# Attention taken as 16 heads by 128 queries instead of 4 heads by 512, with every token tile's projections following it

## The chip, the cores and the metric

One core of a Trainium2 chip. The time is the device time of one execution in microseconds, taken over three runs of the kernel before (2699.6 to 2700.16, median 2700.0).

## The reference

Four residual layers on a sequence of 2048 tokens of width 576 with 32 heads of width 18: A, B, A, B, with the same weights in both rounds.

```python
def _A_ref(x, wq, wk, wv, wo):           # 32 query heads, one key head and one value head
    q = (x @ wq) as [32 heads, 2048, 18]; k = x @ wk; v = x @ wv
    p = softmax(einsum("bhqd,bkd->bhqk", q, k) * 18 ** -0.5)
    return einsum("bhqk,bkd->bhqd", p, v) as [2048, 576] @ wo

def _B_ref(x, wqkv, w_phi, wo):          # linear attention
    q, k, v = x @ wqkv, per head
    phi_q, phi_k = [softmax(q w_phi), softmax(-q w_phi)], the same for k
    kv = sum over the tokens of phi_k^T v;  z = sum over the tokens of phi_k
    return (phi_q kv) / (phi_q z + 1e-6) @ wo

for _ in range(2):
    x = x + _A_ref(layernorm(x)); x = x + _B_ref(layernorm(x))
```

## The kernel before

Each of the two rounds ("layer" 0 and 1 in the code) has three stages.

**Projections of A** (`next_queries`, `project_queries`): queries, keys and values of all tokens; the keys stay in SBUF (`kst`), the values too (`vst`), the queries go to DRAM (`qd`).

**Attention with a stream beside it** (`attend`, L862). A group is 4 heads by 512 queries; 32 groups in all, `NG` = 8 head groups for each of `NC` = 4 chunks of 512 tokens. A group runs over 16 key tiles of 128. For each key tile there are two units: a unit is two score products of TensorE (`score`, L504, two heads at once in two row groups, `sc` in PSUM) and one exp of 128x1024 on ScalarE (L964, `sc` to `pt`). Two units are followed by a sum, four products `pt` by `vst` into a PSUM bank (`add_values`, L800; the profile counts each of the four twice). So one layer has 1024 units and 512 sums. There are three `sc` buffers, and nine `pt`.

The order on TensorE and VectorE is the order in which the program was written: `in_order` (L948) pins both engines. The loop (L1017) has two modes. With work in `bulk` a turn writes three units, the sums that are ready, three more units, then a piece of bulk work (`fill`), then the sums again, unless the piece was heavy (`HEAVY`). Without bulk work it writes two units and one sum at a time. `tick` advances three queues by one step: `urgent` (finishing a group), `loads` (weights) and `slow` (spills of features); a turn with bulk work has three ticks, a free turn one tick for every two units.

Bulk work is B's part: for each chunk, when its last head group is done, `chunk_work` (L1206) multiplies the four token tiles with `wo` (`output`, two halves of 14 products), adds the residual, normalizes and flips each tile through DRAM (`flip_tokens`, `fetch_tokens`, `split_tokens`), and then `mix` takes keys, values and feature queries of each tile with `wk`, `wv` and `wpq` (two halves of 14 products each) and adds to the state (`update_state`, L580). I call such a half, 14 products of 288 columns at L239, a projection: 8 per tile. `wo` and `wpq` share one place in SBUF and are reloaded in turn for each chunk. In layer 0 `fold_phi` runs in the stream as well.

Finishing a group (`finish_group`, L887) takes the group's sums from PSUM (`turned`), divides, transposes back, splits into a high and a low part (`parts`) and packs both with SBUF-to-SBUF transfers into `on`, the stationary operand of the projection with `wo` (`pack`, L827; 4 to 8 transfers). The last group of a chunk then waits three ticks before `chunk_work` starts. Every DMA of the kernel is issued by SyncE (the queue is called SP below), in one order.

**The tail**: the last chunk's tiles. `last_group` finishes the last group with TensorE transposes and packs it, eight projections with `wo` follow (five begun with the products whose operand doesn't come from the last group), four `last_mix`, `finish_state`, and then for all 16 tiles `read_out` and, in layer 0, the projections of the next A.

## Time and profile before

| what | value |
|---|---|
| median of the three runs | 2700.0 us |
| span of the profiled execution | 2699.8 us |
| TensorE, ScalarE, VectorE busy | 2627.5, 2158.1, 1213.9 us |
| granted TensorE clock over the span | 0.994 |
| layer 0: attention to the end of its last sum, about | 136 to 1191 us |
| layer 1: attention to the end of its last sum, about | 1457 to 2517.6 us |
| tail of layer 1 | 2517.6 to 2699.8 us |

The profiled execution's own time is its span; it lies 0.2 us under the median of the runs. In the chain of waits most pieces are TensorE's, some are exps of ScalarE (L964). The rows of a timeline give the start, the length, engine and line, `out<-in`, a count of merged instructions, and in brackets how long the engine stood idle before it and for what. The rows of windows give for each engine the busy time with the number of instructions, then the granted TensorE clock (1.00 is full).

### The profile page before, as it was taken

The numbers are of one execution on the slowest core, as the hardware profiler recorded it, in microseconds if no ns is written. First come the engines' busy times: TensorE is split into PE (matmuls) and PEld (weight loads), VectorE is DVE, ScalarE is ACT, GpSimd is POOL, SyncE is SP. The second block draws the span as 40 slices with busy tenths as digits, with TensorE's granted clock in tenths as the row PEclk, the third lists the DMA queues.
The fourth block names the chain that finished last, engine by engine and source line by source line (L and its number), as shares of the span: only waits on it lengthen the run. The fifth ranks groups of instructions, "written<-read, shape, count | busy, mean of one in ns | idle before, by whom it ended". The sixth has DMA issues, their size and how long they took to land. (4 is left out here: it accounts for less than half of the span.)

```text
span 2699.8 us, 55195 instructions
## 1 busy us (share of the span) xinstructions
PE 2627.5 (97%) x22094; PEld 1444.8 (54%) x22094; DVE 1213.9 (45%) x2807; ACT 2158.1 (80%) x2551; POOL 75.6 (3%) x114
## 2 busy tenths in 40 slices
PE   7999999999999999999999999999999999999999
PEld 6633335453545454558996222455445544554788
DVE  8422244542454245437773111254525452545475
ACT  4599998999899989963335999999998999899421
POOL 1000000000000000002000000000000000000110
PEclk9999999999999999999999999999999999999999
DMA  6531254313421341136645210231224113412354
GB/s 184 163 121 54 65 166 153 93 28 86 119 49 35 84 122 45 38 97 193 185 134 177 71 28 23 55 111 38 58 73 117 41 32 99 118 36 71 108 162 136
DMA packets 353248, 254.30 MB, mean 94 GB/s; under 512 B 191770, under 2 KB 273882, under 8 KB 352986
## 3 DMA queue, kind: packets, MB, share of 16 engines
q1 hardware_dynamic: 352986, 250.71, 32.4%
q8 instruction: 176, 2.88, 0.5%
q14 instruction: 86, 0.70, 0.1%
HBM read 146.12 MB, written 83.69 MB: 85 GB/s over the span
## 5 line engine op out<-in xcount | busy, mean ns | idle before, releaser
L964 ACT ACTIVATE pt<-sc 128x1024 f32<-128x1024 f32 x2036 | 1915.9, 1112 | 155.9 <-PE sc L504 137.2
L504 PE MATMUL sc<-qst,kst 56*128 56x512 f32 x3840 | 712.6, 454 | 16.7 <-ACT pt L964 16.3
L504 PEld LDWEIGHTS sc<-qst,kst 56*128 56x128 f32 x3840 | 324.0, 184 | 618.1 <-ACT pt L964 573.9
L800 PE MATMUL acc<-pt,vst 128*32 128x512 f32 x4096 | 505.1, 599 | 0.0
L800 PE MATMUL ps<-pt,vst 128*32 128x512 f32 x4048 | 491.1, 600 | 1.4 <-DVE featk L536 1.4
L800 PEld LDWEIGHTS ps<-pt,vst 128*32 128x32 f32 x4048 | 105.7, 109 | 212.1 <-issue 206.4
L239 PE MATMUL ps<-wahi,xs 128*128 128x288 f32 x954 | 208.5, 305 | 0.9 <-ACT xs L137 0.7
L800 PEld LDWEIGHTS acc<-pt,vst 128*32 128x32 f32 x4096 | 103.3, 109 | 197.2 <-issue 191.5
L239 PEld LDWEIGHTS ps<-wahi,xs 128*128 128x128 f32 x954 | 157.6, 190 | 11.6 <-issue 3.9
L239 PE MATMUL ps<-walo,xs 128*128 128x288 f32 x530 | 156.2, 297 | 0.0
L889 DVE STREAM_TRANSPOSE turned<-acc 128x512 f32<-128x512 f32 x30 | 21.4, 714 | 217.5 <-PE acc L800 217.5
L388 PE MATMUL ps<-xsc,wbhi 128*128 128x256 f32 x576 | 107.7, 286 | 0.6 <-ACT xsc L137 0.6
L410 ACT ACTIVATE pc<-ps 128x256 fp32r<-128x256 f32 x80 | 30.4, 384 | 93.3 <-PE ps L388 89.2
L239 PEld LDWEIGHTS ps<-walo,xs 128*128 128x128 f32 x530 | 100.6, 190 | 0.0
L263 POOL TENSOR_TENSOR rstd<-var,neghalf 128x1 f32<-128x1 f32 (+1 forms) x56 | 32.0, 571 | 2439.9 <-DVE var L261 2417.7
L137 ACT ACTIVATE xs<-ps 128x512 fp32r<-128x512 f32 x40 | 23.8, 594 | 94.0 <-PE ps L282 93.9
L388 PEld LDWEIGHTS ps<-xsc,wbhi 128*128 128x128 f32 x576 | 91.5, 193 | 1.6 <-ACT xsc L137 1.1
L889 DVE STREAM_TRANSPOSE turned<-ps 128x512 f32<-128x512 f32 x32 | 22.9, 716 | 142.9 <-PE ps L800 142.9
L388 PE MATMUL ps<-xsc,wblo 128*128 128x256 f32 x320 | 86.1, 284 | 0.0
L239 PE MATMUL ps<-wchi,on 128*128 128x288 f32 x378 | 82.2, 303 | 0.0
L296 DVE TENSOR_TENSOR xc<-xc,ps 128x288 f32<-128x288 f32 x58 | 25.7, 445 | 123.4 <-PE ps L239 123.2
L536 DVE COPY featq<-acc 128x288 f32<-128x288 f32 x32 | 14.6, 457 | 123.0 <-PE acc L239 123.0
(257 smaller groups left out, 3200.8 us busy)
## 6 DMA issues: line engine op xcount, KB each, us to landing
qst<-qd SPq DMA_DIRECT2D x360, 72.0 KB
pht<-phi SPq DMA_DIRECT2D x32, 540.0 KB
qd<-pc SPq DMA_DIRECT2D x64, 256.0 KB
on<-parts SPq DMA_DIRECT2D x192, 72.0 KB
phi<-pht SPq DMA_DIRECT2D x96, 144.0 KB
wchi<-wod SPq DMA_DIRECT2D x35, 288.0 KB
wclo<-wod SPq DMA_DIRECT2D x35, 288.0 KB
wchi<-wpqd SPq DMA_DIRECT2D x35, 288.0 KB
```

The costliest lines, as they stand in the source:

```text
L137: A.activation(dst_hi, src, AF.Copy)
L239: T.matmul(dst, xs[:, slot, :], w[half][:, k, c0 : c0 + HALF], start=(n == 0), stop=(n == last))
L263: G.tensor_tensor(rstd, var, neghalf[:, :n], op=ALU.pow)
L296: V.tensor_add(xr, xr, po)
L388: T.matmul(po, lhs, xsc[:, slot, :], start=(n == 0), stop=(n == LASTP))
L410: A.activation(pc[:, 0, :], po, AF.Copy)
L504: T.matmul(sc, kst[head_rows(h), t * P : (t + 1) * P], q[head_rows(h), h // 2, :], start=True, stop=True)
L536: V.tensor_copy(e[:, hs, 0, :], src)
L800: T.matmul(acc[32 * j : 32 * j + 32, :], vst[:, t, :], pts[j], start=first, stop=last)
L889: V.transpose(turned, acc[c, g])
L964: A.activation(pt, sc, AF.Exp, scale=SCALE)
```

## The change

A group is now 16 heads by 128 queries: `NG` = 2 groups for each of 16 token tiles. The products and exps of a group keep their shapes, since four heads stand side by side in the 512 columns that held 512 queries. There are still 32 groups, 1024 units and 512 sums per layer. What differs:

- Query rows are loaded in runs of 128 tokens instead of 512 (`load_queries`, `load_shifts`), in the same number of transfers.
- Finishing a group no longer packs into `on`: `keep_group` writes the parts to DRAM (`od`, 8 transfers), and after a tile's second group `load_heads` reads the whole tile back as `on` (4 transfers), one tick later. Three ticks after that the tile is `finished`.
- `stream` replaces `chunk_work`: for each finished tile the two `wo` projections, the flip, and, once the tokens are there, the six projections of `mix`. When nothing is to be done it sets `idle`, and the loop runs in the free mode.
- `wo`, `wk`, `wv` and `wpq` have a place each, and nothing is reloaded during the attention.
- The last token tile's `wo` and the tiles that are not mixed by the end (`left`; 13, 14 and 15 in layer 0, 14 and 15 in layer 1) stay for the tail. Mixing in the attention starts only with more than `MIX` = 42 units left. So the attention of layer 0 now holds 30 projections with `wo` and 78 of `mix`, that of layer 1 30 and 84; before it was 24 and 72 in each.
- `last_group` packs 16 heads of 128 queries, a head at a time.

```diff
-NG = 8
-GH = H // NG
-NC = 4
+NG = 2
+GH = 4
+HG = H // NG
+HS = HG // GH
+CW = HS * P
...
+    def keep_group(parts, c, g):
+        for j in range(GH):
+            row = first_head(g, j) * DH
+            dst = ods[c % 2][:, row : row + HS * DH, :].rearrange("n (x d) t -> d n x t", d=DH)
+            for n in range(2):
+                nc.sync.dma_start(dst[:, n], parts[32 * j : 32 * j + DH, n, :].rearrange("d (x t) -> d x t", t=P))
+
+    def load_heads(on, c):
+        src = ods[c % 2]
+        for n in range(2):
+            nc.sync.dma_start(on[:, 5 * n : 5 * n + 4, :], src[n, :512].rearrange("(k p) t -> p k t", p=P))
+            nc.sync.dma_start(on[n * 64 : n * 64 + 64, 4, :], src[n, 512:])
...
     def pack(dst, src, g):
         for j in range(GH):
-            row = g * GW + j * DH
+            for x in range(HS):
+                row, cols = (first_head(g, j) + x) * DH, slice(x * P, (x + 1) * P)
...
-        groups = [(c, g) for c in chunks for g in (*range(NG - 2), NG - 1, NG - 2)]
+        groups = [(c, g) for c in range(NT) for g in range(NG)]
...
-                pack(on[c].bitcast(F32), parts.bitcast(F32), g)
-                for _ in range(3):
-                    yield STAGE
-                if g == NG - 2:
-                    bulk.append(after_chunk(c, on[c], Spare(), loads, slow))
+                keep_group(parts.bitcast(F32), c, g)
+                yield STAGE
+                if c == NT - 1 or g == NG - 1:
+                    while c > 0 and c - 1 not in st["added"]:
+                        yield STAGE
+                    on = heads_in()
...
+                    load_heads(on.bitcast(F32), c)
+                    for _ in range(3):
+                        yield STAGE
+                    finished.append((c, on))
...
             while at[0] < len(units):
-                if bulk:
+                if not st["idle"]():
...
                 else:
-                    for n in range(3):
-                        ready = scores(2)
-                        sums(min(ready - 1, done[0] + 2))
-                        tick()
+                    ready = scores(2)
+                    sums(min(ready - 1, done[0] + 2))
+                    tick()
+                    fill()
...
+                def finish_tile():
+                    i, on = finished.popleft()
...
+                    yield from output(i, on, ps)
+                    nc.sync.dma_start(xd[i], xres[i])
...
+                while v.left():
+                    if finished:
+                        yield from finish_tile()
+                    elif fetched is None and unflipped and v.left() > FLIP:
...
+                        flip_tokens(i)
+                        fetched = i, fetch_tokens(i)
+                        if xs is None:
+                            yield from rest(6)
+                            turn_tokens()
+                    elif xs is not None and v.left() > MIX:
...
+                        yield from mix(i, parts, st, ps, spills[layer], loads, slow, turn_tokens)
...
+            EARLY, LATE = range(6), range(6, len(PRODUCTS))
+            sums = [ps.tile([P, HALF], F32, name="ps") for b in range(2)]
+            for b in range(2):
+                run(project(sums[b], st["wo"], b * HALF, on, None, EARLY))
...
+            for b in range(2):
+                run(project(sums[b], st["wo"], b * HALF, on, None, LATE))
+                add_residual(c, b, sums[b])
```

TensorE before, in layer 1, from the last sums of the first chunk's last group (`acc` and `ps` are the two PSUM banks in turn) to the first projection with `wo` (`wchi,on`):

```order
L504 MATMUL sc<-qst,kst 128x512 x4
L800 MATMUL ps<-pt,vst 32x512 x4
L504 MATMUL sc<-qst,kst 128x512 x6
L800 MATMUL ps<-pt,vst 32x512 x8
L504 MATMUL sc<-qst,kst 128x512 x6
L239 MATMUL acc<-wchi,on 128x288
```

The same place after the change, for token tile 2 of layer 1; the row ahead of these is `L797 MATMUL acc`, the tile's last sum:

```order
L797 MATMUL ps<-pt,vst 32x512 x8
L510 MATMUL sc<-qst,kst 128x512 x6
L587 MATMUL acc<-featk,vb_17418 32x36 x32
L797 MATMUL ps<-pt,vst 32x512 x4
L510 MATMUL sc<-qst,kst 128x512 x6
L797 MATMUL ps<-pt,vst 32x512 x8
L510 MATMUL sc<-qst,kst 128x512 x6
L797 MATMUL ps<-pt,vst 32x512 x4
L510 MATMUL sc<-qst,kst 128x512 x6
L797 MATMUL ps<-pt,vst 32x512 x8
L510 MATMUL sc<-qst,kst 128x512 x6
L240 MATMUL acc<-wchi,on 128x288
```

The projection with `wo` now stands 15 units behind the last sum of every tile (`x6` is three units), with the state of the tile before (L587) between them, and it comes 15 times in a layer instead of once for a chunk.

SP's queue before, at the end of a chunk's head groups in layer 1 (`on<-parts` is the packing):

```order
L493 DMA qst<-qd_103 18x2x512 x6
L498 DMA qst<-mxd_105 2x2x512 x2
L836 DMA on<-parts 8x2x512
L839 DMA on<-parts 10x512 x2
L839 DMA on<-parts 18x512 x6
```

And after the change, around the end of a token tile in layer 1 (`od` is the tile's heads in DRAM, `phi<-pht` a spill of features):

```order
L829 DMA od_106<-parts 18x4x128 x8
L494 DMA qst<-qd_103 18x8x128 x6
L501 DMA qst<-mxd_105 2x8x128 x2
L829 DMA od_106<-parts 18x4x128 x8
L642 DMA phi_109<-pht 32x36x32
L834 DMA on<-od_106 128x4x128
L835 DMA on<-od_106 64x128
```

The heads now leave in eight transfers per group and come back in four (the last two rows stand twice in the queue), and a spill stands between the two.

SP's queue before, at the end of layer 0's attention (`on<-xs` packs the layer's last group):

```order
L635 DMA phi_106<-pht 32x36x32 x4
L628 DMA pht<-phi_106 108x10x128
L629 DMA pht<-phi_106 72x128
L836 DMA on<-xs 18x2x512 x4
L202 DMA wclo_13473<-wpqd 128x576
```

The same place after the change:

```order
L635 DMA pht<-phi_108 108x10x128
L636 DMA pht<-phi_108 72x128
L856 DMA on<-xs 10x128
L856 DMA on<-xs 18x128
L853 DMA on<-xs 18x2x128 x9
L853 DMA on<-xs 6x2x128
L853 DMA on<-xs 12x2x128
L853 DMA on<-xs 18x2x128 x2
L853 DMA on<-xs 8x2x128
L856 DMA on<-xs 10x128
L856 DMA on<-xs 18x128 x5
```

The packing of the last group went from 4 transfers to 22. On TensorE all 28 products with `wo` of the last tile stand ahead of the first transposes of `last_mix`.

## Prediction

> **What bounds the kernel now.** I read the page first, for the busy shares and the costliest group:

> ```profile
> PE 2627.5 (97%) x22094; PEld 1444.8 (54%) x22094; DVE 1213.9 (45%) x2807; ACT 2158.1 (80%) x2551; POOL 75.6 (3%) x114
> L964 ACT ACTIVATE pt<-sc 128x1024 f32<-128x1024 f32 x2036 | 1915.9, 1112 | 155.9 <-PE sc L504 137.2
> ```

> The exps fill 1916 us of the 2700, and they wait for scores for 137. So two engines share the bound, and I looked where which one sets the pace. The windows give a stretch with no projections, and the whole attention of layer 1:

> ```profile
> 1500.00:1690.00 190.00, 190.00 (x1248) 54.85 (x1240) 20.95 (x36) 190.00 (x209) 0.00 (x0) 1.00 0.09 25
> 1457.00:2517.60 1060.60, 1050.43 (x8248) 466.53 (x8246) 387.99 (x774) 986.13 (x1070) 6.48 (x12) 1.00 0.26 69
> ```

> In the free stretch ScalarE is never idle: 209 exps in 190 us, 0.909 us a unit. The timeline of ScalarE in a stretch with a projection in every turn, six units to a row:

> ```profile
> 1708.33 5.81 ACT L964 ACTIVATE pt<-sc 128x1024 f32<-128x1024 f32 x6 [0.19 <-PE sc L504]
> 1714.99 5.80 ACT L964 ACTIVATE pt<-sc 128x1024 f32<-128x1024 f32 x6 [0.84 <-PE sc L504]
> 1721.64 5.84 ACT L964 ACTIVATE pt<-sc 128x1024 f32<-128x1024 f32 x6 [0.85 <-PE sc L504]
> ```

> Six units and a projection take 6.65 us (1714.99 to 1721.64) against 5.45 for six free ones, and ScalarE now waits for TensorE. The chain of waits shows what TensorE does in such a turn, and the timeline a turn with a state update (its scores start at 1801.16, the next turn's at 1806.95):

> ```profile
> 1711.74 2.71 PE ps L800 x24
> 1715.35 2.05 PE acc L239 x14
> ```
> ```profile
> 1801.16 0.97 PE L504 MATMUL sc<-qst,kst 56*128 56x512 f32 x6
> 1802.06 0.76 PE L580 MATMUL ps<-featk,vb 128*32 128x36 f32 x63
> 1806.95 0.97 PE L504 MATMUL sc<-qst,kst 56*128 56x512 f32 x6
> ```

> Three sums 2.71 us (0.90 each), a projection 2.05, three scores about 0.90. A projection thus costs the attention 1.20 us, a state 5.79 - 5.45 = 0.34. Layer 1's 1060.6 us are 1024 x 0.909 + 96 x 1.20 + 12 x 0.34 = 1050 and 10 more: hardly a stall is left to remove.

> **More projections in the attention.** 108 + 114 instead of 96 + 96, and 13 + 14 states instead of 12 + 12: 30 x 1.20 + 3 x 0.34 = **+37.0 us**. Two thirds of the way lies beside exps already; 1.20 is what sticks out. A projection directly behind a free stretch isn't shown cleanly; its cost lies between nothing and 1.20, and I take the row's 1.20.

> **The tail has fewer tiles.** The chain at the end of layer 1:

> ```profile
> 2514.25 3.33 PE acc L800 x24
> 2520.55 14.94 PE ps L239 x112
> 2537.95 0.49 ACT xs L137
> 2538.48 9.24 PE ps L239 x56
> 2547.72 0.44 PE ps L282 x4
> 2548.16 0.11 PE ps L286
> 2588.59 0.46 DVE fmax L538
> 2590.07 0.36 DVE kv L586
> 2594.27 2.24 DMA kvb<-featk
> ```

> The last sum ends at 2517.58. The four tiles' mixes run from 2538.48 to 2588.59, 12.5 us a tile. One goes in layer 0, two in layer 1: **-37.6 us**. With fewer tiles side by side each hides less of its chain; I keep the 12.5.

> **The last group is packed in 22 transfers instead of 4.** SP's timeline:

> ```profile
> 2522.49 3.36 SPq L836 DMA_DIRECT2D on<-xs  x4
> ```
> ```profile
> 1543.73 2.12 SPq L493 DMA_DIRECT2D qst<-qd  x6
> 1552.12 3.37 SPq L836 DMA_DIRECT2D on<-parts  x4
> ```

> Before, eight projections (14.94 us) covered the packing, and the mixes began 20.9 us after the last sum. Now only 12 products can run without it, and 28 stand ahead of everything else on TensorE, which stands idle. SP starts 4.91 us after the last sum; 22 x 0.84 = 18.5; the last transfer lands 2.24 later (the kvb row); ten products at 14.94 / 112 = 0.133 make 1.3; then transposes and a copy (0.44 + 0.11 + 0.49) 1.05. That is 28.0, 7.1 later than before, twice: **+14.2 us**. If a transfer takes SP what a `qst` row takes (0.35), it is 17.3, and -7.2 in all.

> **The heads go through DRAM.** This is the new wait. The projection with `wo` is now queued a fixed number of units behind the tile's last sum, and behind it on TensorE stand all scores and sums, for which ScalarE waits. How soon can `on` be there? VectorE's rows for a group that ends in a busy turn, the values of a projection (L567) among them, then the rows of one that ends in a free stretch:

> ```profile
> 2143.73 0.72 DVE L889 STREAM_TRANSPOSE turned<-ps 128x512 f32<-128x512 f32 x1 [1.45 <-PE ps L800]
> 2146.66 0.46 DVE L567 COPY vb<-acc 128x288 f32<-128x288 f32 x1 [1.20 <-PE acc L239]
> 2148.87 0.70 DVE L901 STREAM_TRANSPOSE osb<-turned 128x512 f32<-128x512 f32 x1
> 2150.07 0.69 DVE L140 TENSOR_TENSOR parts<-osb,parts 128x512 fp32r<-128x512 f32 x1
> ```
> ```profile
> 1548.42 0.72 DVE L889 STREAM_TRANSPOSE turned<-ps 128x512 f32<-128x512 f32 x1 [25.67 <-PE ps L800]
> 1551.40 0.69 DVE L140 TENSOR_TENSOR parts<-osb,parts 128x512 fp32r<-128x512 f32 x1
> ```

> A free group has its parts 3.7 us after the last sum. In a busy turn L901 waits for the projection's own work on VectorE (2.2 us, from 2146.66 to 2148.87) and takes 1.9 with the split. Then SP and the way out and back, for which the flip of the tokens is the model:

> ```profile
> 1721.39 2.00 SPq L635 DMA_DIRECT2D flipped<-pht  x4
> 1724.95 0.40 SPq L649 DMA_DIRECT2D xn<-flipped  x1
> 1725.39 1.17 SPq L651 DMA_DIRECT2D xn<-flipped  x2
> ```

> Writes to DRAM at 0.50 each: eight are 4.0. The read was issued 1.56 after the last write's issue ended (1723.39). Four reads, 0.40 + 0.59 twice, 2.0; the last lands 2.2 later. Together 9.8 us from the parts to `on`. At a `qst` row's 0.35 a write it is 8.6, at an `on<-parts` row's 0.84 it is 12.5; the flip's rows are the nearest, since they go the same way.

> By the order (shapes of layer 1):
> - a state between sum and projection (tiles 1, 2, 5, 8, 11, 14): TensorE comes after 1.8 (two sums) + 5.79 + 5.45 + 0.9 = 13.9 us. VectorE waits for the state (3.5), adds it (0.36), splits (1.9): 5.8, with 9.8 and a spill queued ahead of the reads (0.6) 16.2. Wait 2.3.
> - a projection first (tiles 3, 4, 6, 7, 9, 10, 12, 13): TensorE after 0.9 + 6.65 + 5.79 + 0.9 = 14.2; the projection ends at 3.85, with 2.2 + 1.9 the parts are there at 8.0, `on` at 17.8. Wait 3.6.
> - tile 0, free: ten units, 9.1; `on` at 3.7 + 9.8 = 13.5. Wait 4.4.

> Layer 1: 6 x 2.3 + 8 x 3.6 + 4.4 = 47. In layer 0 eight tiles stand so close (4 and 12 like the second kind, 5 and 13 about 3.1, 6 like the third, 0, 1 and 2 behind `fold_phi` about 1, 1 and 3.4): 23; the others have 21 units and more. In hand ScalarE has three units (2.7) against the projection and its next score (2.3): 0.4 of each of the 23 waits is covered. 70 - 9 = **+61 us**.

> **The clock behind such a wait.** The windows around the first mix of the tail:

> ```profile
> 2535.50:2539.20 3.70, 1.70 (x10) 1.28 (x11) 2.99 (x13) 3.13 (x7) 1.66 (x3) 1.00 0.81 219
> 2539.20:2542.60 3.40, 3.40 (x16) 3.40 (x15) 1.12 (x5) 0.60 (x2) 0.54 (x1) 0.50 0.99 351
> ```

> TensorE was busy 1.70 of 3.70 us, and for the next 3.4 its granted clock was 0.50: 1.7 us lost. I count that for the waits of 3.4 and more (9 in layer 1, 4 in layer 0 with its tile 2): 13 x 1.7 = **+22 us**; its bounds are 0 and 23 x 1.7 = 39.

> Against it speaks the end of the mixes: TensorE stood idle through the 2.24 us of the kvb transfer, and the clock behind it stayed full:

> ```profile
> 2596.60:2699.80 103.20, 97.50 (x1254) 93.25 (x1254) 58.96 (x182) 16.06 (x41) 2.33 (x2) 1.00 0.50 156
> ```

> So the size of the gap alone doesn't decide, and 3.4 is my choice between the two.

> [...]

> At nothing I cost the waits for the flipped tokens (14 units, 12.7 us, for 4.1 + 2.0 + 1.6 + 1.6 + 2.2 + 1.6 on VectorE and the way through DRAM, 13.1: 0.4, which the units in hand cover), the finer query loads (29 us ahead of their use) and the weights that aren't reloaded, since no wait for them shows in the 1060.6.

> **The sum**, against the execution's own 2699.8: +37.0 - 37.6 + 14.2 + 61 + 22 = +96.6, so 2796.4; the runs' median is 0.2 above the span, 2796.6.

> **Rivals.**
> - *The clock stays up*: the waits end before half a stretch of 3.4 us is idle, as at the kvb transfer: as forecast without the 22, 2774. [...]
> - *The heads are in time*: `on` within 6.2 us of the parts (14.2 - 8.0). 2699.8 + 13.6 = 2713. For it: the loop has three ticks between read and use. Against it: out and back alone takes 1.56 + 2.2 and twelve issues.
> - *Dear small transfers*: 0.84 on the way out too. 2.7 more for 23 waits, ten more slow windows: 2796 + 62 + 17 = 2875.
> - *TensorE's spare time pays*, the one with a faster end. In free steps it waits for ScalarE, as the row of its weight loads shows:

> ```profile
> 1551.95 0.19 PEld L504 LDWEIGHTS sc<-qst,kst 56*128 56x128 f32 x2 [0.84 <-ACT pt L964]
> ```

>  0.84 for two units, 4.2 for the ten free units of a tile, more than the mean wait of 3.0. If waits fall into it, and the 28 projections that begin behind a free stretch cost nothing instead of 1.20 (34 us), the time is 2713 - 34 = 2679. It decides from the point where a wait and a projection fit into what ScalarE has in hand. Against it: that is three units, 2.7 us, not 4.2.
> - *The weights are still reloaded*: the order has each slab once in a layer, so no chance is kept for it.

> **How the numbers follow.** Chances: forecast 0.38, clock up 0.20, heads in time 0.14, dear transfers 0.08, spare time 0.15, and 0.05 for an end within 0.2%, about what a measurement of this kernel can tell from no change, between the last ones. Slower by over 0.2%: 0.80; within: 0.05; faster: 0.15. The range of 2680 to 2855 leaves out the dear transfers and half of the spare-time case; the forecast's own range is 2760 to 2835 by the bounds of the writes.

> **What would show it.** Waits of TensorE at the first `wo` product of a tile, for a DMA, 2 to 4.5 us long, some 23 of them; granted clock 0.5 after the long ones; 222 projections in the attention, with ScalarE's gaps up by 1.2 for each new one; some 17 us of idle TensorE at the end of each attention; two mixes in layer 1's tail. Wrong I'd be if `on` is there before TensorE, or if the exps don't pause while it waits.

## The result, and the profile after

The changed kernel takes 2848.5 us (four runs, 2847.9 to 2852.8), the kernel before 2700.1 on the same chip: a ratio of 1.055 (95% interval 1.0535 to 1.0565). The forecast was 2796.6 with a range of 2680 to 2855. The sign was right and the time lies in that wide range, but it is 52 us over the forecast and outside the forecast's own range of 2760 to 2835. The profiled execution has a span of 2847.1 us, 147.3 more than that of before.

First the busy shares, ScalarE's group and two groups of projections on the page of the changed kernel (busy time, mean ns; then idle time ahead of them and what ended it):

```profile
PE 2667.7 (94%) x22046; PEld 1474.3 (52%) x22046; DVE 1249.2 (44%) x2852; ACT 2147.3 (75%) x2521; POOL 61.6 (2%) x102
L988 ACT ACTIVATE pt<-sc 128x1024 f32<-128x1024 f32 x2036 | 1920.1, 1047 | 310.5 <-PE sc L510 294.6
L240 PE MATMUL ps<-wahi,xs 128*128 128x288 f32 x1035 | 236.7, 315 | 27.5 <-DVE xs L133 23.7
L240 PE MATMUL acc<-wchi,on 128*128 128x288 f32 x477 | 115.4, 327 | 34.8 <-DMA on<-od 33.9
```

The exps' own time hardly moved (1915.9 to 1920.1), but they wait for TensorE's scores for 295 us instead of 137. TensorE has two new waits: 34 us for the heads (`on`), which was forecast, and 24 us for the flipped tokens (`xs`), which was costed at nothing. The windows of layer 1: attention, the tail up to its first mix, the mixes, the rest:

```profile
1511.90:2680.80 1168.90, 1106.58 (x8635) 516.53 (x8630) 439.79 (x884) 994.03 (x1080) 8.11 (x15) 0.98 0.24 61
2680.80:2708.90 28.10, 10.59 (x42) 8.76 (x42) 5.38 (x14) 1.79 (x5) 1.17 (x2) 0.61 0.19 60
2708.90:2744.70 35.80, 31.99 (x333) 30.55 (x335) 24.28 (x56) 11.70 (x23) 9.30 (x8) 0.88 0.70 213
2744.70:2847.10 102.40, 97.39 (x1232) 93.27 (x1232) 56.34 (x176) 12.79 (x34) 0.00 (x0) 0.97 0.51 157
```

Layer 1's attention, taken here from its first exp (1455.0 before, 1511.9 now), went from 1062.6 to 1168.9 (+106), its tail from 182.2 to 166.3 (-16). In layer 0 the attention grew by 61, and the stretch up to layer 1's first exp fell by 4. Sum: +147.

To see where the 106 and the 61 lie I went through all exps of a layer. By how much the distance from one start to the next exceeds the free unit's 0.909 us is put down to the projection (or state update) that TensorE ran last. The table has these sums in us, with the number of projections; the columns after the second belong to the experiments below. In the traces of both kernels the first six exps of each layer stand under names of weight tiles (`wchi<-sc` to `walo<-sc`); they start 0.90 to 0.92 us apart and add nothing.

| excess over 0.909 a unit | before | changed | e1 | e2 | e3 | e5 | e6 | e8 | e11 |
|---|---|---|---|---|---|---|---|---|---|
| layer 1, first `wo` projections (15) | - | 44.0 | 44.1 | 89.6 | 18.9 | 64.1 | 40.2 | 25.3 | 42.2 |
| layer 1, first mix projections (14) | 13.2 (12) | 74.4 | 108.4 | 16.8 | 67.7 | 17.2 | 52.7 | 15.9 | 41.2 |
| layer 1, all | 130.5 | 236.5 | 272.3 | 222.6 | 204.3 | 198.4 | 209.2 | 156.4 | 200.2 |
| layer 0, all | 147.5 | 208.7 | 206.3 | 208.1 | 191.8 | 190.9 | 207.8 | 185.2 | 209.6 |

Layer 1 adds up: 130.5, 18 more projections and two states (22.3), 44.0 - 15 x 1.20 = 26 at the heads, 74.4 - 14 x 1.20 = 58 at the tokens: 236. So more than half of layer 1's loss lies at a place that the forecast had at nothing.

A tile with such a wait. VectorE, SP and TensorE of the changed kernel (each row: start, length, then in brackets the idle time before it and its end):

```profile
1913.17 0.72 DVE L907 STREAM_TRANSPOSE turned<-ps 128x512 f32<-128x512 f32 x1 [7.50 <-PE ps L797]
...
1916.14 0.69 DVE L134 TENSOR_TENSOR parts<-osb,parts 128x512 fp32r<-128x512 f32 x1
1916.75 0.42 DVE L133 CAST xs<-xn 128x512 fp32r<-128x512 f32 x1
```
```profile
1909.33 0.39 SPq L656 DMA_DIRECT2D xn<-flipped  x1
1909.76 2.10 SPq L658 DMA_DIRECT2D xn<-flipped  x2
```
```profile
1917.32 0.37 PE L240 MATMUL ps<-wahi,xs 128*128 128x288 f32 x1 [2.38 <-DVE xs L133]
...
1920.53 1.65 PE L510 MATMUL sc<-qst,kst 56*128 56x512 f32 x6
```

The tokens' reads are issued by 1911.86. But VectorE works in written order, to which `in_order` pins it, and the split of the tokens is written behind the finishing of the head group: it idles 7.50 us until the group's last sum, takes 3.6 for the group, and only then turns to the tokens. And the projection takes 3.2 us to the next scores, not 2.05, most of it the clock's doing (with the clock kept up it is 2.5, e4 below). Three windows around the wait:

```profile
1912.00:1915.40 3.40, 2.94 (x22) 0.69 (x20) 2.13 (x4) 3.40 (x5) 0.00 (x0) 1.00 0.36 105
1915.40:1918.80 3.40, 1.35 (x8) 1.14 (x9) 2.82 (x7) 0.74 (x1) 0.00 (x0) 0.99 0.19 47
1918.80:1922.20 3.40, 3.40 (x18) 2.38 (x21) 1.49 (x4) 0.77 (x1) 0.00 (x0) 0.51 0.47 128
```

TensorE was busy 1.35 of 3.40 us, and the next window runs at half clock (0.51).

### The profile page after: what moved, and what is told of

Its sections match the earlier page's. It is cut to its first block, busy times and chain, and to the rows that moved or that the text cites. A ratio compares the mean times of both kernels' runs of the same rounds, so it can differ in the third digit from the quotient of the medians.

```text
span 2847.1 us, 55572 instructions
## 1 busy us (share of the span) xinstructions
PE 2667.7 (94%) x22046; PEld 1474.3 (52%) x22046; DVE 1249.2 (44%) x2852; ACT 2147.3 (75%) x2521; POOL 61.6 (2%) x102
## 5 line engine op out<-in xcount | busy, mean ns | idle before, releaser
L988 ACT ACTIVATE pt<-sc 128x1024 f32<-128x1024 f32 x2036 | 1920.1, 1047 | 310.5 <-PE sc L510 294.6
L797 PE MATMUL acc<-pt,vst 128*32 128x512 f32 x4096 | 498.6, 602 | 6.1 <-DVE xc L297 3.3
L797 PE MATMUL ps<-pt,vst 128*32 128x512 f32 x4048 | 497.0, 603 | 0.0
L240 PE MATMUL ps<-wahi,xs 128*128 128x288 f32 x1035 | 236.7, 315 | 27.5 <-DVE xs L133 23.7
L797 PEld LDWEIGHTS acc<-pt,vst 128*32 128x32 f32 x4096 | 107.3, 109 | 226.7 <-issue 214.7
L797 PEld LDWEIGHTS ps<-pt,vst 128*32 128x32 f32 x4048 | 105.9, 110 | 215.4 <-issue 210.9
L240 PEld LDWEIGHTS ps<-wahi,xs 128*128 128x128 f32 x1035 | 177.2, 197 | 55.9 <-issue 25.2
L240 PE MATMUL ps<-walo,xs 128*128 128x288 f32 x575 | 174.5, 305 | 0.0
L240 PE MATMUL acc<-wchi,on 128*128 128x288 f32 x477 | 115.4, 327 | 34.8 <-DMA on<-od 33.9
L297 DVE TENSOR_TENSOR xc<-xc,acc 128x288 f32<-128x288 f32 x53 | 23.9, 451 | 252.8 <-PE acc L240 252.8
L240 PEld LDWEIGHTS acc<-wchi,on 128*128 128x128 f32 x477 | 83.2, 202 | 59.5 <-issue 25.9
L240 PEld LDWEIGHTS ps<-walo,xs 128*128 128x128 f32 x575 | 113.6, 198 | 0.0
L240 PE MATMUL ps<-wbhi,xs 128*128 128x288 f32 x486 | 107.0, 305 | 0.0
L574 DVE COPY vb<-ps 128x288 f32<-128x288 f32 x44 | 20.1, 458 | 186.2 <-PE ps L240 186.2
L240 PEld LDWEIGHTS ps<-wbhi,xs 128*128 128x128 f32 x486 | 79.6, 188 | 16.1 <-issue 15.7
```

What stands on the lines that cost most here:

```text
L240: T.matmul(dst, xs[:, slot, :], w[half][:, k, c0 : c0 + HALF], start=(n == 0), stop=(n == last))
L297: V.tensor_add(xr, xr, po)
L797: T.matmul(acc[32 * j : 32 * j + 32, :], vst[:, t, :], pts[j], start=first, stop=last)
L988: A.activation(pt, sc, AF.Exp, scale=SCALE)
```

## The experiments

All are edits of the changed kernel, timed beside the kernel before. Theory A: TensorE's waits for heads and tokens, with the clock behind them, are the loss. Rivals: the waits only change places; the flip's way through DRAM is too long by itself; something else of the tail or the queries costs.

**e1: query loads with the eighth key tile.**

```diff
-if t == 0 and hh == 0 and 0 < n < len(groups) - 1:
+if t == 8 and hh == 0 and 0 < n < len(groups) - 1:
```

> Of the changed kernel only the place moves where a group's query loads are issued: with the group's eighth key tile, not with its first; the order on TensorE is the same, row for row. Queue theory: in layer 1 ten of fourteen tiles keep TensorE waiting 1.9 to 3.0 us at their first mix product (excess over ScalarE's pace about 6.0 us each), because the eight query loads (some 2.9 us of SP) and the writes of the heads stand between the flip's writes and its reads; in the four tiles where they stand behind, the wait is 0.66 and the excess 3.2. Without the loads in the way the ten come down to the four: 10 x 2.8 = 28 us less, about 2820 (2812 to 2830). Path theory (the rival): the flip's own way through DRAM is longer than the twelve units that are left to it, whatever else SP does: the waits stay and the time is 2848 within 5.

Measured: 2877.5 (ratio 1.066, 1.064 to 1.067), 29 slower. Both expectations fell. SP and TensorE in a tile of e1:

```profile
1906.89 1.99 SPq L642 DMA_DIRECT2D flipped<-pht  x4
1909.66 0.28 SPq L494 DMA_DIRECT2D qst<-qd  x1
1917.31 0.27 SPq L829 DMA_DIRECT2D od<-parts  x1
1917.76 0.38 SPq L656 DMA_DIRECT2D xn<-flipped  x1
```
```profile
1921.30 0.58 PE L240 MATMUL ps<-wahi,xs 128*128 128x288 f32 x1 [5.19 <-DVE xs L133]
```

With the loads moved, a write of the heads stands ahead of the tokens' reads in SP's order. It waits for VectorE's parts, and SP stands for 7.4 us with the reads behind it. The edit hadn't only taken something out of the queue; it changed what stands where.

**e2: a tile is mixed when the next tile's tokens have been asked for.**

```diff
-elif xs is not None and v.left() > MIX:
+elif xs is not None and v.left() > MIX and (fetched is not None or v.left() < FLIP):
...
-yield from wait(lambda: not finished and v.left())
+yield from wait(lambda: not finished and v.left() and not (xs is not None and MIX < v.left() < FLIP))
```

> A tile is mixed only when the next tile's tokens have been asked for (or when under 84 units are left), so a tile's flip runs beside the mix of the tile before; the tiles left for the tail stay 13, 14, 15 and 14, 15, and the order changes in layer 1 alone. Theory that the flipped tokens are the largest unforeseen cost: the fourteen first mix projections of layer 1, which now take 74 us beyond ScalarE's pace, fall to 14 x 1.2 to 1.6 = 17 to 22: 52 to 57 less, 2791 to 2797. Rival: TensorE's waits only move to the first wo product, which comes nearer to its heads, and the time stays above 2830.

Measured: 2829.6 (1.048, 1.046 to 1.050), 19 less. The waits for tokens are gone, and those for heads grew, as the same two groups on e2's page show:

```profile
L240 PE MATMUL ps<-wahi,xs 128*128 128x288 f32 x801 | 175.8, 306 | 2.4 <-ACT xs L131 1.5
L240 PE MATMUL acc<-wchi,on 128*128 128x288 f32 x459 | 118.2, 343 | 59.8 <-DMA on<-od 58.6
```

Both were partly right: 58 us gained at the tokens (74.4 to 16.8, 1.20 each), 46 given back at the heads (44.0 to 89.6). The expectations of e5 and e8 count fourteen of the fifteen `wo` projections there, without tile 1's, and so have 42, and 62 for e5's 64.1.

**e3: heads later.** Three ticks more between the reads of `on` and the `wo` projections.

```diff
-                    for _ in range(3):
+                    for _ in range(6):
```

> Six ticks instead of three between the reads of the heads and the tile's wo projections, so TensorE comes about six units (5.5 us) later. By the trace of the changed kernel the first wo products cost 44 us beyond ScalarE's pace in layer 1 (15 of them; 18 without a wait) and, with their waits of 1.2 to 5.0, some 27 too much in layer 0: if the heads are the whole of it, 2848 - 26 - 27 = 2795 (2785 to 2810). By the forecast's own size of that term (61 + 22 for the clock) it would be 2766. Rival: the later wo pushes the flip into other transfers and the wait comes back there: within 10 of 2848.

Measured: 2799.3 (1.037, 1.035 to 1.039), 49 less, as theory A had it. On e3's page the group waits no longer:

```profile
L240 PE MATMUL acc<-wchi,on 128*128 128x288 f32 x423 | 94.7, 309 | 3.0 <-DVE xc L297 3.0
```

With the 7 us that it also spared at the tokens (74.4 to 67.7), the heads cost some 43 us, clock included: 26 in layer 1 and 17 in layer 0 (208.7 to 191.8; TensorE's waits for `on` there are 16.8 in all), not the forecast's 83.

**e4: the wait filled.** Fourteen products ahead of the first mix projection of nine tiles of layer 1: `i % 3` leaves out tiles 0, 3, 6, 9 and 12, where the expectation counts ten tiles.

```diff
     def project(dst, w, c0, xs, ...):
+        for _ in range(st.pop("warm", 0)):
+            T.matmul(dst, w[0][:, 0, 0:P], w[0][:, 0, 0:HALF], start=True, stop=True)
...
+                        if layer == 1 and i % 3:
+                            st["warm"] = 14
```

> In layer 1, ahead of the first mix product of ten tiles (all but 3, 6, 9 and 12), fourteen products more into the same PSUM bank, weights by weights, whose result is overwritten at once: TensorE works (14 x 0.133 = 1.9 us) where it stood idle for 1.9 to 3.0. Clock theory: the stretch of 3.4 us behind such a wait, at a granted clock of 0.5, costs 1.7 us each, and comes because TensorE stood idle: ten projections take 2.1 us again instead of 3.1 to 3.8 and the time falls by 10 to 17, to 2831 to 2838. [...]

Measured: 2835.1 (1.051, 1.049 to 1.053), 13.5 less, in the middle of what the clock theory gave. The windows of the same tile, 4, in e4, and TensorE's rows:

```profile
1905.50:1908.90 3.40, 3.40 (x25) 2.15 (x24) 3.23 (x6) 2.87 (x4) 0.00 (x0) 1.00 0.14 43
1908.90:1912.30 3.40, 2.95 (x19) 2.29 (x19) 1.84 (x6) 0.00 (x0) 0.00 (x0) 1.00 0.35 84
```
```profile
1907.10 2.11 PE L239 MATMUL ps<-wahi 128*128 128x288 f32 x14
1909.45 0.41 PE L242 MATMUL ps<-wahi,xs 128*128 128x288 f32 x1 [0.25 <-DVE xs L133]
...
1911.98 0.97 PE L512 MATMUL sc<-qst,kst 56*128 56x512 f32 x6
```

The wait itself is as long as before, TensorE only works through it; the clock stays at 1.00 and the projection takes 2.5 us to the scores. So it went in eight of the nine filled tiles; in the changed kernel all nine had a window at half clock. At these tiles half clock thus came from TensorE's idle time.

That the total came out in the middle is partly luck. The nine filled projections cost 7.6 us less (56.0 to 48.4 beyond ScalarE's pace; the eight that kept the clock 1.05 each, not 1.7). The rest came where nothing was filled: 4.6 at the `wo` projections (44.0 to 39.4), 1.3 at tile 0's mix and 2.2 at the layer's start, with a mean granted clock of 0.975 for 0.968 over the span.

**e5: e2 and e3 together**, both diffs above.

> The two edits at once: the heads' three ticks more, and a tile mixed only when the next one's tokens are asked for. The heads alone measured 49 less. In that run the first mix products of layer 1 still cost 67.7 us beyond ScalarE's pace; mixed a tile later they cost 16.8. If the two add up: 2799 - 51 = 2748 (2740 to 2760). Rival: one wait takes the place of the other again, as when the later mix alone gave 42 of its 58 us back at the heads: above 2785.

Measured: 2789.6 (1.034, 1.032 to 1.036). The two don't add up: of the 51 us expected beside e3, 10 came. By the rows of a tile of e5, VectorE now has the finished mix of the tile before (L555 to L639) ahead of the heads' parts, and TensorE waits again:

```profile
1908.70 0.75 DVE L555 TENSOR_REDUCE fz<-featq 128x32 f32<-128x576 f32 x1
...
1912.50 1.38 DVE L639 STREAM_TRANSPOSE pht<-featq 128x1152 f32<-128x1152 f32 x1
...
1914.97 0.69 DVE L134 TENSOR_TENSOR parts<-osb,parts 128x512 fp32r<-128x512 f32 x1
```
```profile
1922.13 0.37 PE L240 MATMUL acc<-wchi,on 128*128 128x288 f32 x1 [1.09 <-DMA on<-od]
```

**e6: the tokens' split ahead of the group's finishing.**

```diff
-                            yield from rest(6)
+                            yield from rest(3)
                             turn_tokens()
+                            yield from rest(3)
```

> VectorE's split of the flipped tokens is written three ticks after their reads, not six, so that it stands ahead of the finishing of the head group and not behind it; TensorE's order is the same. VectorE theory: in most tiles of layer 1 the tokens have landed but VectorE, which works in written order, first waits for the group's last sum and finishes the group (turned to parts, 3.7 us). Then the waits of 2.4 at the first mix product go to nearly nothing in eight of the ten tiles and to nothing in the four: 8 x 4.4 + 4 x 1.6 = 42 less, 2800 to 2815. Queue theory: what is late is the read itself, behind query loads or the heads' writes on SP: TensorE's waits stay above 2 us and the time is 2848 within 8.

Measured: 2822.1 (1.045, 1.044 to 1.047), 26 less: VectorE's order is a part, but a smaller one than expected (74.4 to 52.7). In tiles 2, 5, 8 and 11, which still wait for 1.3 to 3.5, SP is late; tile 8 in e6:

```profile
2185.49 0.32 SPq L642 DMA_DIRECT2D flipped<-pht  x1
2185.90 2.32 SPq L494 DMA_DIRECT2D qst<-qd  x6
2188.26 0.59 SPq L501 DMA_DIRECT2D qst<-mxd  x2
2188.89 1.43 SPq L642 DMA_DIRECT2D flipped<-pht  x3
2192.88 0.38 SPq L656 DMA_DIRECT2D xn<-flipped  x1
```
```profile
2196.72 0.40 PE L240 MATMUL ps<-wahi,xs 128*128 128x288 f32 x1 [2.00 <-DVE xs L133]
```

The next group's eight query loads stand between the flip's first write and its other three. Tiles 0, 6 and 9 also keep waits of 1.2 to 2.2.

**e11: e1 and e6 together**, both diffs above.

> The two edits that gave 26 us less (the split of the tokens ahead of the group's finishing) and 29 us more (query loads with the eighth key tile) at once; TensorE's order is that of the changed kernel. SP's order has now the four flip writes, two query loads and then the reads in every tile of layer 1; with the query loads moved alone it had the heads' first write, which waits for VectorE's parts, ahead of the reads, and with the split alone it had all eight query loads between the flip's writes in tiles 2, 5, 8 and 11. Queue theory: what stands on SP ahead of the reads decides, so the 29 us were the write that waits, and nothing against the move itself: the four tiles lose their waits too (excess 3.0 to 6.7 to some 2), 12 less than the split alone, 2810 (2802 to 2817). Rival: the later query loads are themselves what costs (they come too late or collide with something else): above 2835.

Measured: 2811.2 (1.041, 1.039 to 1.043), 37 less than the changed kernel, where e1 alone was 29 more. The write that waits no longer stands ahead of the reads:

```profile
2183.98 2.02 SPq L642 DMA_DIRECT2D flipped<-pht  x4
2186.09 0.79 SPq L494 DMA_DIRECT2D qst<-qd  x2
2187.80 0.39 SPq L656 DMA_DIRECT2D xn<-flipped  x1
```

So the late query loads did no harm in e1; SP's order did. With both orders mended the path is nearly short enough: nine of fourteen first mix products wait for 0.2 us or less. Tiles 0, 6 and 9 still wait for 1.5 to 1.9, and no run took these waits away with the mix left in its place.

**e7: the last group through DRAM, in 14 transfers.** `last_group` calls `keep_group` and reads the 16 heads back with 6 transfers.

```diff
...
-            pack(on.bitcast(F32), parts.bitcast(F32), NG - 1)
+            keep_group(parts.bitcast(F32), NT - 1, NG - 1)
+            load_last_heads(on.bitcast(F32), NT - 1)
```

> The last head group of each layer goes through DRAM (8 writes, 6 reads) as the others do, not in 22 transfers from SBUF to SBUF (16.8 us of SP at 0.77 each in the changed kernel). 8 x 0.41 + about 1 + 6 x 0.5 + 2.9 to land = 10.2 us against 16.8 + 2.5 = 19.3. If the packing is what the tail waits for: 9 less in each layer, 18 in all, 2830 (2826 to 2835). Rival: something else is as late (the weights that the tail loads, the residuals): 2848 within 4.

Measured: 2823.9 (1.047, 1.044 to 1.050), 25 less. SP in the tail of the changed kernel, then in e7's:

```profile
2685.80 1.65 SPq L856 DMA_DIRECT2D on<-xs  x2
2687.49 11.40 SPq L853 DMA_DIRECT2D on<-xs  x14
2698.94 4.54 SPq L856 DMA_DIRECT2D on<-xs  x6
```
```profile
2671.93 3.25 SPq L829 DMA_DIRECT2D od<-xs  x8
...
2677.73 0.45 SPq L848 DMA_DIRECT2D on<-od  x1
```

17.6 us of issue became 6.3 from the first write to the last read, and of the 28.1 us up to the first mix product 16.8 are left: 11 less in each layer. The stretch after layer 0 fell by 10.4, layer 1's tail by 14.2.

**e10: one tile more in layer 1's tail.** In layer 1 mixing stops at 120 units left, not 42.

```diff
-elif xs is not None and v.left() > MIX:
+elif xs is not None and v.left() > (MIX if layer == 0 else 120):
```

> The changed kernel with layer 1's tile 13 mixed in the tail (mixing in the attention stops at 120 units left). By the forecast's prices a mix in the attention is 6 x 1.20 + 0.34 = 7.5, one in the tail 12.5; the first mix product of tile 13 now also waits (5.9 instead of 1.2): 12.5 - 7.5 - 4.7 = nothing, 2848 within 4, with the attention 12 shorter and the tail 12.5 longer. Rival: in a tail of few tiles the chains no longer hide behind one another, so a tile more costs the tail nearly nothing: 2838 or less.

Measured: 2852.5 (1.057, 1.055 to 1.059), 4 more, with ranges of the runs that overlap: no change, as expected. Attention and tail of layer 1 in e10:

```profile
1512.00:2670.80 1158.80, 1099.30 (x8489) 503.67 (x8489) 422.69 (x855) 990.86 (x1076) 8.86 (x16) 0.97 0.24 61
2670.80:2848.50 177.70, 151.31 (x1770) 143.96 (x1768) 97.33 (x272) 33.02 (x74) 15.16 (x14) 0.90 0.47 145
```

A mix in the tail is 11.4 us (177.7 - 166.3), in the attention 10.1 with its wait (1168.9 - 1158.8), for the 12.5 and the 12.2 (7.5 and a wait of 4.7) of the expectation.

**e8: e5 with eight ticks, and e7.** The diffs of e2 and e7, and:

```diff
-                    for _ in range(3):
+                    for _ in range(8):
```

> Eight ticks between the reads of the heads and the wo projections (not three, and not six as before), a tile mixed only when the next one's tokens are asked for, and the last group through DRAM. With six ticks the two later edits left 62 us at layer 1's first wo products, twelve of them still with a wait of 1.6 to 3.0; two ticks more put four to five units (some 4 us) ahead of each, and the two tiles that had no wait cost 2.1. If only lateness was left: 2789.6 - (62 - 14 x 2.1 = 33) - 24.7 (measured for the tail) = 2732 (2725 to 2742). Rival: VectorE's or SP's backlog grows with the delay and the waits stay: 2760 or more.

Measured: 2728.4 (1.011, 1.009 to 1.012), 120 less than the changed kernel, 4 off the sum. Layer 1's attention in e8:

```profile
1482.00:2571.00 1089.00, 1077.74 (x8636) 500.50 (x8633) 438.74 (x884) 994.70 (x1080) 8.10 (x15) 1.00 0.26 65
```

TensorE is busy for 1077.7 of 1089.0 us at full clock. Against the 1062.6 of before that is +26.4, of which 22.3 are the 18 projections and two states more. Hardly a wait is left to take there; what remains is work. What can still be won lies in layer 0: by the table its attention has 37.7 more than before, 23 of them beyond its twelve projections and one state more, and e8 is 28 behind the kernel before.

**e9: e8 with the tail's idle time filled.** 32 products more, into a bank that nothing reads.

```diff
+            spin = ps.tile([P, HALF], F32, name="ps")
+            for _ in range(32):
+                T.matmul(spin, st["wo"][0][:, 0, 0:P], st["wo"][0][:, 0, 0:HALF], start=True, stop=True)
```

> The same kernel with 32 products more (weights by weights, into a bank that nothing reads) in each layer's tail, where TensorE stands idle for some 4.8 us until the last heads arrive; behind that gap the products took 0.24 us each, not 0.13, for some 9 us. Clock theory: with TensorE busy the clock stays up and each tail is some 4 us shorter: 8 less than the kernel without, about 2724. Rival: the clock isn't what the tail waits for, or the added work delays the first real products: no gain, or up to 4 us more.

Measured: 2725.6 (1.009, 1.007 to 1.011) beside e8's 2728.4; the ranges of their runs overlap, so this is inconclusive. The clock held through the gap (1.00) and fell right behind it (0.54), where TensorE waits for the last transfers and the transposes (windows of e9's tail):

```profile
2582.50:2585.90 3.40, 2.49 (x14) 1.63 (x12) 0.00 (x0) 0.00 (x0) 0.00 (x0) 1.00 0.33 94
2585.90:2589.30 3.40, 2.16 (x9) 1.68 (x8) 2.04 (x5) 1.11 (x2) 0.62 (x1) 0.54 0.69 196
```

No version beat the kernel before.

## Why the prediction was right in kind and 52 us short

- **More projections, +37.0: right.** Six units and a projection still take 6.65 us, as ScalarE's timeline shows (1795.94 to 1802.59), and layer 1's accounts close with 1.20 each. (That two thirds of a projection lie beside exps is a slip: of its 2.05 us 0.85 do.)

```profile
1795.94 5.61 ACT L988 ACTIVATE pt<-sc 128x1024 f32<-128x1024 f32 x6 [1.11 <-PE sc L510]
1802.59 5.79 ACT L988 ACTIVATE pt<-sc 128x1024 f32<-128x1024 f32 x6 [1.05 <-PE sc L510]
```

  The projection right behind a free stretch costs more than the 1.20 taken: 1.6 to 2.2 where it has no wait (2.1 in e8's first tiles, 2.2 at e11's first mixes). So the rival by which TensorE's spare time pays falls.
- **Fewer mixes and the packing, -37.6 + 14.2 = -23.4: right.** Measured -19.9 (-4.0 and -15.9). The 28.0 us up to the first mix were 28.1; a transfer took 0.80 for 0.84, and a tile less saved 11.4 for 12.5.
- **Heads through DRAM, +61, with the clock +83: the mechanism was right, the term too large.** They cost 43 (e3). A steady tile of the changed kernel, SP's rows and TensorE's wait inside the first `wo` projection:

```profile
1815.11 3.27 SPq L829 DMA_DIRECT2D od<-parts  x8
1819.27 0.39 SPq L834 DMA_DIRECT2D on<-od  x1
```
```profile
1823.48 0.54 PE L240 MATMUL acc<-wchi,on 128*128 128x288 f32 x2 [0.79 <-DMA on<-od]
```

  A write takes SP 0.41, not 0.50, and the reads begin 0.9 behind the last write, not 1.56; so `on` is some 1 us late here, not 2.3 to 3.6. The rivals of the dear transfers (0.84 a write) and of heads that are in time fall with these rows.
- **The clock, +22: right in kind, its size by luck.** Beside four in the first 18 us of layer 1's, twenty-five windows of 3.41 us at half clock lie in the two attentions. Two come while the weights are folded and 23 behind waits, against the thirteen counted: nine behind waits for heads, ten for tokens, four for VectorE. A window cost less than the 1.7 taken: 1.05 at the eight tiles where e4 kept the clock up. At that price, an estimate, 23 cost 24 us, which is part of the other terms here. The rival without them, 2774, falls with these windows and with e4.
- **The flipped tokens, costed at nothing: this step failed.** It compared the path's own 13.1 us with 12.7 and left 0.4 to the units in hand. The path was alone in that sum. On VectorE the split stands behind the finishing of the group (e6), on SP the flip shares the queue with the next group's query loads and the heads' writes (e6's tile 8, e11). The query loads had been dismissed because they come 29 us ahead of their use; what counted was who stands behind them. The cost was 58 us in layer 1, the clock's part included. Some 14 of them are no waiting: a first mix without a wait still costs 2.2 in e11, 1.0 more than 1.20, where it stands behind a free stretch; in e2, right behind a projection, it costs 1.20. In layer 0 no first mix waits for its tokens.
- **Open:** of layer 0's 46 us beyond its projections (208.7 - 147.5 - 14.7) the heads are 17. In the other 29 what shows clearest is that TensorE waits for VectorE in three places (5.0, 3.3 and 2.7 us), where VectorE is held up by a spill, by a finished mix, and by the finishing of a group with a tile's normalization. The longest:

```profile
686.04 0.61 PE L240 MATMUL acc<-wahi,xs 128*128 128x288 f32 x1 [5.02 <-DVE featk L543]
```

  No run took these away alone, so that part is argued and not shown.

By terms: 37.0 - 19.9 + 43 at the heads + 58 at the tokens + 29 open = 147. The 52 us are therefore a difference of larger errors: heads and clock were 40 too large, and the tokens with layer 0's open part, 87 together, were at nothing.

## What to carry to other kernels

A hand-over that crosses several engines was as late here as the queues on its way (29 us more in e1, 26 less in e6, 37 less in e11), not as its own steps: list for every engine and DMA queue what is written ahead of it, and what that waits for. When a wait goes, ask what is written next behind it: two edits that each took a wait away (49 and 19 us) gave 59 together, and two ticks more for the heads, with the tail's 25 taken off, another 36. And moving TensorE's work could gain here only where TensorE stood idle: with layer 1's waits nearly gone (TensorE busy for 1077.7 of 1089.0 us), e8 is still 28 us behind the kernel before.

## What the runs showed of the hardware

In these rows, of pieces of 18 partitions or fewer, SP paid 0.80 us for a transfer from SBUF to SBUF (17.6 for 22 in the changed kernel's tail) and 0.41 for one from SBUF to DRAM (3.25 for 8 in e7).
